# Loads of three pairs on two queues, weights behind the first x, and the second pair transposed before the FFN

## The chip, the cores and the metric

The kernel runs on one core of a Trainium2 chip. A core has TensorE (matmuls, PE in the profile), VectorE (DVE), ScalarE (ACT), GpSimd (POOL) and SyncE (SP); each works through its own instructions in order and they meet by semaphores. Loads and stores go through 16 DMA engines; SP and ACT issue them on hardware queues, GpSimd on a software queue. The metric is the device time of one execution in microseconds (us); lower is better.

## The reference

A state-space scan (Mamba-2 form) is followed by a feed-forward network (FFN). The scan works on x (4 batches, 8 heads, 768 positions, 32 dims), decays a, and B and C with 16 states. Per head, in chunks of positions:

```python
L = np.exp(cum[:, :, :, None] - cum[:, :, None, :]) * causal
M = np.einsum('bhin,bhjn->bhij', Cc, Bc) * L
y = np.einsum('bhij,bhjd->bhid', M, xc) + np.einsum('bhin,bhnd->bhid', Cc, state) * exp(cum)
state = decay_full * state + np.sum(Bx, axis=2)
```

The result, seen as 3072 tokens of 256 features, goes through the FFN with w_in (256 x 2048) and w_out (2048 x 256):

```python
h = np.maximum(x @ w_in, 0.0)
return h * h @ w_out
```

## The kernel before

The work is cut into 12 pairs. A pair is one batch and 256 positions of all 8 heads, two chunks of 128 positions (u = 0, 1); `PAIRS` runs over the four batches first, so that pairs 0 to 3 are the first 256 positions of the four batches. The decays are scanned into prefix products once at the start (`P_sb`, its reciprocal `Pinv`, and the totals `Ptot`), and the factors are multiplied into C and x: C times the prefix product is `cz`, x times its reciprocal is `xs`.

One pair goes through these steps, each a small function: `ph_load` (DMAs of C, B and x; rows of 128 bytes for B and C, 256 for x), `prep_c`, `prep_b`, `prep_x` (`cz`, the bf16 copy `Bb`, and `xs`; `ph_prep` does all three on GpSimd), `ph_tr` (six transposes on TensorE into PSUM, then one copy to `bct`), `ph_mt` (16 matmuls C times B), `ph_mask` (four multiplications by the causal mask on VectorE, into `mts`), `ph_u` (16 matmuls for the chunk's new state), `ph_s` (states S of the two chunks, on VectorE), `ph_y` (40 or fewer matmuls into Y, then the copy to `T`, bf16). For pair 0 the copy to T is split in two, one half on ScalarE and one on VectorE.

A pair's T is one block of 256 tokens of the FFN. A block has eight steps; a step is `mm1` (four 256-column matmuls with w_in, ReLU on ScalarE into `hb`), `square` (VectorE, one step later) and `mm2` (four matmuls with w_out, `LAG` = 4 steps later). `steps` lists all 96 steps. `at(s, fn, ...)` hangs a pair's functions on a step; within a step the order is mm1, dummy matmuls in the first steps, the functions hung there, square, mm2. From pair 4 on the schedule is regular, eight steps a pair. Pairs 1 to 3 have their steps in `first_steps`, as (tr, u, s, mt, four masks, y), and the first 16 steps interleave blocks 0 and 1 (`head`).

The order on every engine is the order in which the code is written out (`manual_schedule`). Before the loop the code goes: the early loads, dummy matmuls (`warm`, which compute nothing that is used), the decay scan, all of pair 0, the preparation of pair 1. The weights come in eight transfers on GpSimd's queue, each a quarter of w_in (`load_wi`, L125) or w_out (`load_wo`, L130), cast to bf16. Three things order the loads:

- the queue: SP issues a, C0, x0, C1, B1, x1, then pairs 2 and later; ACT issues the constants `cf` and B0;
- `touch` copies on GpSimd (L403, L430): a tiny copy whose input is awaited, so that the weight loads behind it in the queue leave later. L403 waits for `P_sb`, L430 for C of pair 2;
- `gate=True` in `ph_load`: GpSimd writes one element of each destination first, so that the DMA waits for GpSimd to get there.

PSUM has three pools of two buffers each: `ps_h` (tag hps: FFN hidden, and in the start U of pair 0), `ps_o` (tag ops: FFN output, dummies, transposes of pair 0), `ps_s` (tag A: the scan). A buffer is taken again when the last reader of its earlier content is done.

Of the kernel before, what the change touches and what calls it, by code (L numbers as in the profile page):

```python
# [30 lines left out]
def kernel(  # L31
# [14 lines left out]
    nc = tc.nc  # L46
# [64 lines left out]
    def ph_load(k, order="CBx", eng=None, gate=False):  # L111
        b, j = PAIRS[k]
        t = loaded.setdefault(k, {})
        for what in order:
            src, w = {"B": (B, N), "C": (C, N), "x": (x, D)}[what]
            dst = nat.tile([128, NH, 2 * w], FP32, tag=f"{what}_nat", name=f"{what}_nat{k}")
            if gate:
                nc.gpsimd.memset(dst[:, 0, 0:1], 0.0)
            (eng or nc.sync).dma_start(  # L119
                out=dst, in_=_dap(src, (b * NH * S + j * 256) * w,  # L120
                                  [[2 * w, 128], [S * w, NH], [1, 2 * w]]))
            t[what] = dst
# [6 lines left out]
    def load_wo(f0, f1):  # L129
        nc.gpsimd.dma_start(  # L130
            out=w_out_b[:, f0:f1, :],
            in_=moe_w_out[f0 * 128:f1 * 128, :].rearrange("(f p) d -> p f d", p=128))
# [24 lines left out]
    def prep_x(k, eng):  # L157
        b, j = PAIRS[k]
        xs = prep.tile([128, 2, 256], BF16, tag="xs", name=f"xs{k}")
        eng.tensor_tensor(  # L160
            out=_fap(xs, 0, [[256, 2], [32, 8], [1, 32]]),
            in0=_fap(loaded[k]["x"], 0, [[32, 2], [64, 8], [1, 32]]),
            in1=_fap(Pinv, b * 24 + j, [[96, 2], [3, 8], [0, 32]]), op=ALU.mult)
        live.setdefault(k, {})["xs"] = xs
# [7 lines left out]

    def ph_tr(k):
        v = live[k]
        pool, tag = (ps_o, "ops") if k < 1 else (ps_s, "A")
        tr = pool.tile([128, 2, 3, 128], BF16, tag=tag, name=f"tr{k}",
                       padded_shape=[128, 2, 4, 128] if k < 1 else [128, 4, 4, 128])
        for r in range(2):
            nc.tensor.transpose(tr[:, r, 0, :], v["Bb"][:, r, :], eye_b)  # L179
            for g in range(2):  # L180
                nc.tensor.transpose(tr[:, r, 1 + g, :], v["cz"][:, r, 112 * g:112 * g + 128], eye_b)  # L181
        bct = big.tile([128, 2, 3, 128], BF16, tag="bct", name=f"bct{k}")
        nc.vector.tensor_copy(out=bct, in_=tr)  # L183
        v["bct"] = bct

    def ph_mt(k):
# [15 lines left out]
    def ph_mask(k, q, src=None):  # L202
        v = live[k]
        nc.vector.tensor_tensor(  # L204
            out=v["mts"][:, q], in0=v["mt"][q // 2][:, q % 2] if src is None else src,
            in1=_fap(cb, 128, [[128, 2], [0, 2], [1, 128]]), op=ALU.mult)
# [157 lines left out]
    with tc.manual_schedule():  # L364
        nc.sync.dma_start(out=a_nat, in_=_dap(a, 0, [[256, 96], [1, 256]]))
        nc.scalar.dma_start(out=cf, in_=cf_d.ap())
        ph_load(0, "C")
        ph_load(0, "B", nc.scalar)
        ph_load(0, "x")
        nc.gpsimd.dma_start(out=cb, in_=cb_d.ap())  # L370
        load_wi(0, 4)
        ph_load(1)

        nc.vector.memset(dum, 0.0)  # L374
        nc.vector.memset(zer, 0.0)
        for i in range(3):
            nc.vector.memset(cz[i], 0.0)
        dps = ps_o.tile([128, 256], FP32, tag="ops", name="dps", padded_shape=[128, 512])

        def warm(n, cols=256):  # L380
            for _ in range(n):
                nc.tensor.matmul(dps[:, 0:cols], dum[:, 0:128], dum[:, 0:cols],  # L382
                                 start=True, stop=True, skip_group_check=True)

        warm(18)
        nc.vector.tensor_scalar(out=a_cl, in0=a_nat, scalar1=1e-6, scalar2=1.0, op0=ALU.max, op1=ALU.min)
        for u in range(2):
            nc.vector.tensor_tensor_scan(out=cp_r[:, u * 128:(u + 1) * 128], data0=a_cl[:, u * 128:(u + 1) * 128],
                                         data1=zer, initial=1.0, op0=ALU.mult, op1=ALU.add)
        nc.vector.tensor_tensor(out=pick_p, in0=_fap(pick, 0, [[0, 2], [1, 12]]),  # L390
                                in1=_fap(cp_r, 127, [[128, 2], [0, 12]]), op=ALU.mult)
        ptr = ps_h.tile([128, 2, 96], FP32, tag="hps", name="ptr", padded_shape=[128, 2, 256])
        for r in range(2):
            nc.tensor.transpose(ptr[:, r, :], _fap(cp_r, r, [[2, 128]]), eye_f)
        warm(1)
        pps = ps_h.tile([128, 2, 12], FP32, tag="hps", name="pps", padded_shape=[128, 2, 256])
        nc.tensor.matmul(pps, spread, pick_p, start=True, stop=True)
        nc.scalar.copy(out=P_sb, in_=ptr)
        prep_b(0, nc.scalar)
        nc.scalar.copy(out=Ptot, in_=pps)  # L400
        prep_c(0, nc.vector)
        nc.vector.reciprocal(out=_fap(Pinv, 0, [[96, 2], [3, 32]]), in_=_fap(P_sb, 0, [[96, 2], [3, 32]]))
        nc.gpsimd.tensor_copy(out=touch, in_=P_sb[:, 0, 0:1])  # L403
        load_wi(4, 8)
        load_wo(0, 4)
        prep_x(0, nc.gpsimd)
        load_wi(8, 12)
        load_wo(4, 8)
        warm(4, 128)
        ph_tr(0)  # L410
        warm(8, 128)
        ph_mt(0)
        warm(6, 128)
        mtc = big.tile([128, 2, 2, 2, 128], BF16, tag="mtc", name="mtc", bufs=1)
        for i in (1, 0):
            nc.scalar.copy(out=mtc[:, i], in_=live[0]["mt"][1][:, i])
        ph_mask(0, 0)
        warm(8, 128)
        ph_u(0)
        warm(8, 128)  # L420
        ph_mask(0, 1)
        ph_mask(0, 3, mtc[:, 1])
        ph_mask(0, 2, mtc[:, 0])
        ph_s(0, (0,))
        prep_b(1, nc.scalar)
        prep_c(1, nc.vector)
        prep_x(1, nc.gpsimd)
        load_wo(8, 12)
        ph_load(2, gate=True)
        nc.gpsimd.tensor_copy(out=touch, in_=loaded[2]["C"][:, 0, 0:1])  # L430
        load_wi(12, 16)
        load_wo(12, 16)
        ph_load(3, gate=True)
        ph_y(0)
        warm(9, 128)
        ph_s(0, (1,))

        head = ([(0, f) for f in range(6)] + [(1, f) for f in range(6)]
                + [(0, 6), (1, 6), (0, 7), (1, 7)])
        steps = head + [(b, f) for b in range(2, NPAIR) for f in range(8)]  # L440
        todo = {}

        def at(s, fn, *args):
            todo.setdefault(max(s, 0), []).append((fn, args))

        def recip_rest():
            nc.vector.reciprocal(out=_fap(Pinv, 1, [[96, 2], [3, 32], [1, 2]]),
                                 in_=_fap(P_sb, 1, [[96, 2], [3, 32], [1, 2]]))

        at(7, recip_rest)  # L450
        first_steps = {
# [3 lines left out]
        for k in range(1, NPAIR):  # L455
            s0 = 8 * k - LEAD
            if k == 2:
                at(8, prep_c, k, nc.gpsimd)
                at(10, prep_b, k, nc.scalar)
                at(9, prep_x, k, nc.gpsimd)  # L460
            elif k == 3:
                at(13, ph_prep, k)
            elif k > 3:
                at(s0 - (8 if k == 4 else 15), ph_load, k)
                at(s0 - (4 if k == 4 else 7), ph_prep, k)
            if k in first_steps:
                tr, uu, st, mt, ms, yy = first_steps[k]
                at(uu, ph_u, k)
            else:
                tr, st, mt, ms, yy = s0, s0 - 1, s0 + 2, (s0 + 2, s0 + 3, s0 + 3, s0 + 4), s0 + 6  # L470
            at(tr, ph_tr, k)
            at(mt, ph_mt, k)
            for q in range(4):
                at(ms[q], ph_mask, k, q)
            at(st, ph_s, k)
            at(yy, ph_y, k)
        for s in range(len(steps) + LAG):
            if s < len(steps):
                mm1(*steps[s])
            if 1 <= s < LAG:  # L480
                warm(4, 128)
            for fn, args in todo.pop(s, []):
                fn(*args)
            if 1 <= s < len(steps) + 1:
                square(*steps[s - 1])
            if LAG <= s < len(steps):
                mm2(*steps[s - LAG])
        mm2_last(NPAIR - 1, [f for _, f in steps[len(steps) - LAG:]])
# [30 lines left out]
```

## Time and profile before

| | |
|---|---|
| median of 13 runs | 126.67 us (125.59 to 128.28) |
| the profiled execution | 127.09 us, its span 125.3 us |
| TensorE busy | 115.4 us, 92% of the span |
| VectorE, ScalarE, GpSimd busy | 85.7, 72.8, 31.8 us |
| granted TensorE clock, mean | 0.979 |
| loads of C, B, x on SP, from issue to landing (median) | 4.0, 4.1, 4.4 us |
| w_in and w_out, a quarter each | 5.6 and 6.3 us |
| first FFN matmul | 11.38 us |
| `ph_mt` of pair 4, 5, 6 | 43.68, 52.40, 61.13 us |

The span runs from the first to the last instruction of the profiled execution; its own time has 1.79 us beside that. "Granted clock" is the share of full speed that TensorE's throttle allowed. A timeline line gives start, duration, engine, line, operation, output and input, count, and in brackets how long the engine had stood still before it and what ended that. A line of the chain of waits gives start, length and the work. A line of the windows gives the stretch and its length, busy time of PE, weight loads, DVE, ACT and POOL with counts, the granted clock, the DMA share and GB/s.

### The profile page before, as it was taken

The page shows a single profiled execution, that of the slowest core. Times are in us where ns is not written, and L with a number is a line of the kernel's source. Part 1 is how long each engine was busy: PE and PEld are TensorE (multiplying, and loading weights), DVE is VectorE, ACT ScalarE, POOL GpSimd, SP SyncE. Part 2 cuts the span into 40 slices and gives each one's busy share as a digit, 9 for nine tenths or more (in the row PEclk, how much of TensorE's full clock was granted, in tenths as well). Part 3 has the DMA queues.
Part 4 walks back from the last instruction along what each step waited for, and adds up shares of the span by engine and source line. Part 5 has one row for each costly group of instructions (what it writes and reads, how often), then busy time and mean ns, then how long its engine had stood idle before and what let it go on. Part 6 is the DMA issues. An engine that isn't in the chain of part 4 may idle for free.

```text
span 125.3 us, 4310 instructions
## 1 busy us (share of the span) xinstructions
PE 115.4 (92%) x1814; PEld 93.0 (74%) x1814; DVE 85.7 (68%) x207; ACT 72.8 (58%) x131; POOL 31.8 (25%) x61
## 2 busy tenths in 40 slices
PE   6779889859999999999999999999999999999970
PEld 4558668636667888788788788887887897788840
DVE  3486896519599798696797794874956947934520
ACT  4244555613557558567485585576575765867720
POOL 5184502803691060250330420602400000000000
PEclk9999999995999999999999999999999999999997
DMA  4999997799854724707505607229020020010211
GB/s 84 200 195 171 193 120 139 75 157 187 156 106 159 130 59 107 148 4 154 102 0 133 123 35 154 67 88 166 8 86 8 0 86 5 14 70 5 84 42 42
DMA packets 42804, 12.10 MB, mean 97 GB/s; under 512 B 37824, under 2 KB 41360, under 8 KB 42784
## 3 DMA queue, kind: packets, MB, share of 16 engines
q1 hardware_dynamic: 38240, 9.28, 34.5%
q0 software_dynamic: 3248, 2.20, 13.4%
q10 hardware_dynamic: 1296, 0.35, 1.7%
q8 instruction: 14, 0.23, 0.8%
q14 instruction: 6, 0.05, 0.1%
HBM read 10.77 MB, written 3.15 MB: 111 GB/s over the span
## 4 chain that ended last, share of the span: by engine, by line
PE 72%; DMA 15%; SPq 4%; DVE 3%; POOL 2%; ACT 1%; issue 1%; DVEq 0%; POOLq 0%
PE ops L336 30%; PE hps L316 29%; DMA x_nat<-in_x_dram 7%; DMA w_in_b<-in_moe_w_in_dram 4%; DMA C_nat<-in_C_dram 4%; SPq L119 3%; PE Y L256 3%; PE mt L193 3%; PE Y L284 2%; PE tr L181 2%; DVE h L326 2%; PE U L222 1%; PE ops L349 1%; DVE mts L204 1%; POOL xs L160 1%
## 5 line engine op out<-in xcount | busy, mean ns | idle before, releaser
L320 ACT ACTIVATE hb<-hps 128x512 bf16<-128x512 f32 x96 | 57.5, 599 | 39.0 <-PE hps L316 38.2
L316 PE MATMUL hps<-T,w_in_b 128*128 128x256 bf16 x384 | 58.6, 276 | 2.8 <-DMA w_in_b<-in_moe_w_in_dram 2.4
L336 PE MATMUL ops<-w_out_b,h 128*128 128x256 bf16 x368 | 56.2, 276 | 0.0
L326 DVE TENSOR_TENSOR h<-hb 128x512 bf16<-128x512 bf16 x96 | 39.7, 437 | 7.4 <-ACT hb L320 7.4
L316 PEld LDWEIGHTS <-w_in_b 128*128 128x128 bf16 x384 | 37.5, 99 | 8.5 <-DMA w_in_b<-in_moe_w_in_dram 2.8
L336 PEld LDWEIGHTS <-h 128*128 128x128 bf16 x368 | 34.0, 99 | 6.5 <-issue 2.0
L204 DVE TENSOR_TENSOR mts<-mt,cb 128x512 bf16<-128x512 f32 x46 | 30.2, 682 | 10.3 <-PE mt L193 10.3
L140 POOL TENSOR_TENSOR cz<-C_nat,P_sb 128x256 bf16<-128x256 f32 x10 | 6.7, 669 | 38.8 <-DMA C_nat<-in_C_dram 23.1
L160 POOL TENSOR_TENSOR xs<-x_nat,Pinv 128x512 bf16<-128x512 f32 x12 | 12.8, 1064 | 8.0 <-DMA x_nat<-in_x_dram 6.8
L183 DVE COPY bct<-tr 128x768 bf16<-128x768 bf16 x12 | 6.7, 557 | 10.4 <-PE tr L181 10.3
L382 PE MATMUL dps<-dum 128*128 128x128 bf16 (+1 forms) x74 | 8.2, 261 | 1.1 <-DVE dum L374 1.1
L382 PEld LDWEIGHTS <-dum 128*128 128x128 bf16 x74 | 6.0, 109 | 2.3 <-DVE dum L374 1.1
L305 ACT CAST T<-Y 128x512 bf16<-128x512 f32 x11 | 6.4, 585 | 0.7 <-PE Y L256 0.3
L361 ACT COPY osb<-ops 128x512 f32<-128x512 f32 x11 | 6.4, 580 | 0.4 <-PE ops L336 0.4
L154 POOL CAST Bb<-B_nat 128x128 bf16<-128x128 f32 x18 | 5.2, 315 | 1.3 <-DMA B_nat<-in_B_dram 1.3
L181 PE MATMUL tr<-cb,cz 128*128 128x128 bf16 x48 | 5.3, 220 | 0.0
L193 PE MATMUL mt<-bct 32*64 32x256 bf16 x192 | 5.1, 280 | 0.2 <-DVE bct L183 0.2
L245 DVE TENSOR_SCALAR S<-z,Ptot 128x64 bf16<-128x64 f32 x16 | 4.7, 296 | 0.6
L179 PE MATMUL tr<-cb,Bb 128*128 128x128 bf16 x24 | 4.8, 220 | 0.3 <-ACT Bb L152 0.3
L256 PE MATMUL Y<-mts,xs 64*32 64x128 bf16 x384 | 5.0, 219 | 0.0
L244 DVE TENSOR_TENSOR z<-U,S 128x64 f32<-128x64 f32 x16 | 3.6, 224 | 1.9 <-PE U L222 1.4
L284 PE MATMUL Y<-bct,S 32*32 32x128 bf16 x160 | 4.4, 217 | 0.2 <-DVE S L241 0.2
(45 smaller groups left out, 45.2 us busy)
## 6 DMA issues: line engine op xcount, KB each, us to landing
x_nat<-in_x_dram SPq DMA_DIRECT2D x12, 256.0 KB, 4.4
out_dram<-osb SPq DMA_DIRECT2D x11, 256.0 KB, 2.6
C_nat<-in_C_dram SPq DMA_DIRECT2D x12, 128.0 KB, 4.0
B_nat<-in_B_dram SPq DMA_DIRECT2D x11, 128.0 KB, 4.1
w_in_b<-in_moe_w_in_dram POOLq DMA_DIRECT2D x4, 256.0 KB, 5.6
w_out_b<-in_moe_w_out_dram POOLq DMA_DIRECT2D x4, 256.0 KB, 6.3
B_nat<-in_B_dram ACTq DMA_DIRECT2D x1, 128.0 KB, 4.8
out_dram<-osb ACTq DMA_DIRECT2D x1, 128.0 KB, 1.7
```

The lines of the kernel that those rows point to most:

```text
L140: eng.tensor_tensor(out=_fap(czk, 0, [[240, 2], [32, 8], [1, 16]]), in0=_fap(loaded[k]["C"], 0, [[16, 2], [32, 8], [1, 16]]), in1=_fap(P_s ...
L160: eng.tensor_tensor(out=_fap(xs, 0, [[256, 2], [32, 8], [1, 32]]), in0=_fap(loaded[k]["x"], 0, [[32, 2], [64, 8], [1, 32]]), in1=_fap(Pinv ...
L181: nc.tensor.transpose(tr[:, r, 1 + g, :], v["cz"][:, r, 112 * g:112 * g + 128], eye_b)
L193: nc.tensor.matmul(mt[q // 2][64 * u:64 * u + 64, q % 2, r, :, :], bct[32 * q:32 * q + 32, r, 0, u * 64:u * 64 + 64], _fap(bct[32 * q:32 * ...
L204: nc.vector.tensor_tensor(out=v["mts"][:, q], in0=v["mt"][q // 2][:, q % 2] if src is None else src, in1=_fap(cb, 128, [[128, 2], [0, 2], ...
L256: nc.tensor.matmul(Y[u][32 * q:32 * q + 32, g, :], v["xs"][64 * u:64 * u + 64, r, h * 32:h * 32 + 32], v["mts"][64 * u:64 * u + 64, q, r, ...
L284: nc.tensor.matmul(Y[u][32 * q:32 * q + 32, g, :], S_b[32 * q:32 * q + 32, g * 32:(g + 1) * 32], _fap(v["bct"][32 * q:32 * q + 32], 128 + ...
L316: nc.tensor.matmul(hps[:, i, :], w_in_b[:, g, f * 128:(f + 1) * 128], T[blk][:, g].rearrange("p r u t -> p (r u t)"), start=(g == 0), stop ...
L320: nc.scalar.activation(out=hb, in_=hps, func=AF.Relu)
L326: nc.vector.tensor_tensor(out=h2, in0=hb, in1=hb, op=ALU.mult)
L336: nc.tensor.matmul(ops[blk][:, r, :], h2[:, i, r * 128:(r + 1) * 128], w_out_b[:, f, :], start=(f == 0 and r == 0), stop=(f == 15), skip_g ...
L382: nc.tensor.matmul(dps[:, 0:cols], dum[:, 0:128], dum[:, 0:cols], start=True, stop=True, skip_group_check=True)
```

## The change

Three places change.

The loads: B and x of pair 1 move from SP's queue to ACT's. The loads of pair 2 follow C of pair 1 on SP at once, with neither gate nor touch. On GpSimd `prep_x(0)` takes the place of the first touch, so that the second weight transfer and all later ones stand behind it; `prep_x(1)` stands behind w_in 8:12, and the last four weight transfers follow it without a touch between them.

Pair 1: `prep_c(1)` on VectorE stands directly behind the copy of pair 0's transposes, `prep_b(1)` on ScalarE behind the copies of pair 0's mt, and `ph_tr(1)` stands before `ph_y(0)`, in a buffer of `ps_h`; ScalarE makes its copy to `bct`. Both states of pair 0 are made before Y.

The steps: pair 1's mt and masks come one step earlier, pair 2's functions four, pair 3's one. `head` interleaves after five steps of block 0 and not six. Pair 2 is prepared whole on GpSimd at step 3. The dummy matmuls change in number.

```diff
     def ph_tr(k):
         v = live[k]
-        pool, tag = (ps_o, "ops") if k < 1 else (ps_s, "A")
+        pool, tag = [(ps_o, "ops"), (ps_h, "hps")][k] if k < 2 else (ps_s, "A")
...
-        nc.vector.tensor_copy(out=bct, in_=tr)
+        if k == 1:
+            nc.scalar.copy(out=bct, in_=tr)
+        else:
+            nc.vector.tensor_copy(out=bct, in_=tr)
...
         load_wi(0, 4)
-        ph_load(1)
+        ph_load(1, "C")
+        ph_load(1, "B", nc.scalar)
+        ph_load(1, "x", nc.scalar)
+        ph_load(2)
...
-        nc.gpsimd.tensor_copy(out=touch, in_=P_sb[:, 0, 0:1])
+        prep_x(0, nc.gpsimd)
         load_wi(4, 8)
         load_wo(0, 4)
-        prep_x(0, nc.gpsimd)
         load_wi(8, 12)
-        load_wo(4, 8)
         warm(4, 128)
         ph_tr(0)
+        prep_c(1, nc.vector)
         warm(8, 128)
         ph_mt(0)
-        warm(6, 128)
+        warm(8, 128)
         mtc = big.tile([128, 2, 2, 2, 128], BF16, tag="mtc", name="mtc", bufs=1)
         for i in (1, 0):
             nc.scalar.copy(out=mtc[:, i], in_=live[0]["mt"][1][:, i])
+        prep_b(1, nc.scalar)
         ph_mask(0, 0)
-        warm(8, 128)
         ph_u(0)
-        warm(8, 128)
+        warm(10, 128)
         ph_mask(0, 1)
         ph_mask(0, 3, mtc[:, 1])
         ph_mask(0, 2, mtc[:, 0])
-        ph_s(0, (0,))
-        prep_b(1, nc.scalar)
-        prep_c(1, nc.vector)
+        ph_s(0)
         prep_x(1, nc.gpsimd)
+        load_wo(4, 8)
         load_wo(8, 12)
-        ph_load(2, gate=True)
-        nc.gpsimd.tensor_copy(out=touch, in_=loaded[2]["C"][:, 0, 0:1])
         load_wi(12, 16)
         load_wo(12, 16)
         ph_load(3, gate=True)
+        ph_tr(1)
         ph_y(0)
         warm(9, 128)
-        ph_s(0, (1,))
-
-        head = ([(0, f) for f in range(6)] + [(1, f) for f in range(6)]
-                + [(0, 6), (1, 6), (0, 7), (1, 7)])
+
+        head = ([(0, f) for f in range(5)] + [(1, f) for f in range(4)]
+                + [(0, 5), (1, 4), (1, 5), (0, 6), (1, 6), (0, 7), (1, 7)])
...
-            1: (0, 3, 4, 1, (1, 1, 2, 2), 5),
-            2: (11, 14, 14, 12, (12, 12, 13, 13), 15),
-            3: (16, 19, 20, 17, (17, 18, 18, 19), 21)}
+            1: (None, 2, 3, 0, (0, 0, 1, 1), 4),
+            2: (7, 10, 10, 8, (8, 8, 9, 9), 11),
+            3: (15, 18, 19, 16, (16, 17, 17, 18), 20)}
...
             if k == 2:
-                at(8, prep_c, k, nc.gpsimd)
-                at(10, prep_b, k, nc.scalar)
-                at(9, prep_x, k, nc.gpsimd)
+                at(3, ph_prep, k)
             elif k == 3:
-                at(13, ph_prep, k)
+                at(11, ph_prep, k)
...
-            at(tr, ph_tr, k)
+            if tr is not None:
+                at(tr, ph_tr, k)
...
-            if 1 <= s < LAG:
-                warm(4, 128)
+            if 2 <= s < LAG:
+                warm(3, 128)
```

More of the change, by code (lines that the diff above doesn't have):

```diff
@@ L174, in ph_tr @@
         v = live[k]
-        pool, tag = (ps_o, "ops") if k < 1 else (ps_s, "A")
+        pool, tag = [(ps_o, "ops"), (ps_h, "hps")][k] if k < 2 else (ps_s, "A")
         tr = pool.tile([128, 2, 3, 128], BF16, tag=tag, name=f"tr{k}",
-                       padded_shape=[128, 2, 4, 128] if k < 1 else [128, 4, 4, 128])
+                       padded_shape=[128, 2, 4, 128] if k < 2 else [128, 4, 4, 128])
         for r in range(2):
```

## The prediction

> **What bounds the kernel now.** I read the page first, then the chain of waits, then windows, then the timeline of the first 45 us.
>
> ```profile
> span 125.3 us, 4310 instructions
> PE 115.4 (92%) x1814; PEld 93.0 (74%) x1814; DVE 85.7 (68%) x207; ACT 72.8 (58%) x131; POOL 31.8 (25%) x61
> PEclk9999999995999999999999999999999999999997
> ```
>
> TensorE sets the time, except in one slice of granted clock, the tenth (28.2 to 31.3 us). In the chain of waits, the matmuls of L193 recur every 8.7 us from 43.68 on with little but matmuls between them: one pair of the steady loop.
>
> ```profile
> 15.76 5.10 DMA C_nat<-in_C_dram
> 21.44 5.13 DMA w_in_b<-in_moe_w_in_dram
> 26.61 0.61 PE hps L316 x4
> ...
> 43.68 0.35 PE mt L193 x16
> ...
> 52.40 0.35 PE mt L193 x16
> ```
>
> The change ends before that loop, so 125.3 - 43.68 = 81.6 us stay and only the instant of `ph_mt(4)` can move. The windows up to it (PE busy is the second figure, granted clock the third from last):
>
> ```profile
> 11.38:18.64 7.26, 6.36 (x123) 4.78 (x124) 5.94 (x15) 4.17 (x7) 2.00 (x5) 1.00 1.14 164
> 18.64:24.61 5.97, 5.97 (x54) 4.88 (x53) 3.23 (x7) 3.87 (x8) 3.44 (x8) 1.00 0.73 111
> 24.61:26.61 2.00, 0.00 (x0) 0.00 (x1) 0.49 (x2) 0.00 (x0) 0.07 (x1) 1.00 1.06 117
> 28.00:31.50 3.50, 3.50 (x34) 2.24 (x32) 3.20 (x8) 1.19 (x2) 1.23 (x4) 0.52 1.00 179
> ```
>
> TensorE stands for 2.00 us, then works 3.5 us at clock 0.52, which loses 0.48 x 3.50 = 1.68 us. The timeline has the reason: the last quarter of w_in is issued at 21.44 because GpSimd's touch copy waited for C_nat2.
>
> ```profile
> 20.98 0.26 POOL L430 COPY touch<-C_nat 128x1 f32<-128x1 f32 x1 [5.18 <-DMA C_nat<-in_C_dram]
> 26.61 0.61 PE L316 MATMUL hps<-T,w_in_b 128*128 128x256 bf16 x4 [2.00 <-DMA w_in_b<-in_moe_w_in_dram]
> ```
>
> **The change, part by part** (pN is pair N; times from the span's start).
>
> *The stall.* The touch and the gate of p2's loads go; p2's loads are issued early on SP, and w_in 12:16 follows the other weights. GpSimd's queue in order: x_nat0 lands at 1.66 + 6.5 = 8.2, `xs0` runs about 8.35 to 9.4 (row: 1.06), then issues of 0.75 each: w_in 4:8 at 9.45, w_out 0:4 at 10.2, w_in 8:12 at 10.95, `xs1` to 12.9, then four more to 16. w_in 12:16 leaves at about 14.4. With the landings of before (4.7 to 6.8 us for a weight) it lands at 19 to 21, and behind its predecessors at their slowest spacing (2.4 us, 13.2 to 15.6) at about 23.5. Step 12, which reads it, comes at about 27.7 (step 6 at 21.3, worked out below, six steps of 8 x 0.109 and 1.2 for p2's tr, mt and U). The 2.00 us go, and with them the cause of the 1.68 us. Next late is nothing of the weights, by little: w_in 4:8 lands at 9.45 + 4.8 = 14.25, used at 15.75; w_in 8:12 at 10.95 + 6.3 = 17.25, used at 17.55. C2, B2 and x2, behind C1 on SP, compete with w_in 4:8 as C1, B1 and x1 did before. The hold itself costs nothing under that cover; without it, 0.5 us (6.8 for w_in 4:8) to 1.6 us (8.2, the longest early landing, for w_in 8:12).
>
> *Where the new wait sits.* `prep_c(1)` moves on VectorE from behind p0's masks to before them. In before:
>
> ```profile
> L119 SPq DMA_DIRECT2D C_nat<-in_C_dram x1: 1004/1004/1004, 2.3 to 2.3; - x1
> DMA to landing us min/median/max: 6.7/6.7/6.7
> 6.89 0.56 DVE L183 COPY bct<-tr 128x768 bf16<-128x768 bf16 x1
> 7.98 1.29 DVE L204 TENSOR_TENSOR mts<-mt,cb 128x512 bf16<-128x512 f32 x2 [0.54 <-PE mt L193]
> 9.19 0.76 DVE L204 TENSOR_TENSOR mts<-mtc,cb 128x512 bf16<-128x512 bf16 x2
> ```
>
> C_nat1 lands at 2.28 + 6.7 = 9.0, while the masks begin at 7.98. VectorE runs in order: masks, S0, half of T0 and the whole FFN now queue behind C_nat1. It still stands behind x_nat0 on SP. Lower bound: 9.0, since what leaves its way (w_in 4:8 and w_out 0:4, issued at 6.33 and 7.04) is replaced by B1 and x1 on ACT. By bytes: about 1454 KB had moved by 9.0; now a, cf, C0, B0, cb, x0, w_in 0:4, C1 (1176 KB), B1 (128) and most of x1 (170 to 256) make 1474 to 1560 KB, at 200 KB/us 9.1 to 9.5. Upper bound: all of B1 and x1 on top at the rates of the steady loop's loads, alone on their queue (about 160 GB/s for B, 0.8 us; 240 for x, 1.1 us): 10.9. I take 9.4, nearest the byte count, because several queues together held 200 GB/s here.
>
> A page bears on this. The Trainium skill ("DMA: Bandwidth & Descriptors", Rules for kernel authors) says that spreading DMAs over SP, ACT and GpSimd saves only issue time, as all share 16 engines. That speaks against a gain from the second queue; the near-equal landings of C0 on SP (3.9 us) and B0 on ACT (4.8 us) agree, and by it C1 would land no earlier than the byte count has it.
>
> *ACT's issues.* SP's first four issues took 0.39, 0.43, 0.58 and 1.00. ACT's four (cf, B0, B1, x1) then end near 3.3, its table load (1.28) at 4.6, before `P_sb` at 5.57. At the worst early row (2.38 for x1) `P_sb` is 0.4 late, hidden behind C_nat1; uncovered, 0.4.
>
> *From C_nat1 to the first FFN matmul.* `prep_c(1)` 9.45 to 9.86 (0.41); four masks as before (7.98 to 9.95) to 11.95; S_0 0.27 to 12.25. `ph_tr(1)` now stands on PE ahead of `ph_y(0)` and takes the "hps" buffer of U0, free only after S_0: tr 0.40, to 12.75; Y0 0.5. ACT copies bct1 ahead of its half of T0: 768 columns, extrapolated from 0.37 (256) and 0.58 (512), are 0.80, 12.95 to 13.75, then T0 0.37; first matmul of step 0 at about 14.25. Before it was 11.38: **+2.87**. Bounds +2.3 (no wait for the buffer, C1 at 9.0) to +4.4 (C1 at 10.9).
>
> *Steps 0 to 5.* tr1 and bct1 are done, so p1's masks start at t0 + 0.95 and run 2.6, two squares 0.84, S 0.27, Y1 at t0 + 4.75, T1, step 5 at 6.15, step 6 at t0 + 7.05. Before, step 6 began at 18.64 = 11.38 + 7.26: **-0.2**. Six dummy matmuls of 0.06 fewer are inside this; the other added ones run in waits. `prep_b(1)` is earlier on ACT, behind the mtc copies, and B_nat1 (9.6 before) is in by then; `ph_prep(2)` is on GpSimd from about 16.3 to 18.6, for step 7 at about 22.
>
> *Steps 6 to 24.* The matmul work is the same. p2 ends at step 11 instead of 15: the 0.28 before `tr2` and the 0.2 for T2 go, while `recip_rest` (0.95), now ahead of bct2 on VectorE, may hold mt2 by 0.2: **-0.3** (0 to -0.5).
>
> *A new cold stretch.* PE is idle 8.35 to 9.45 and, after U0 and ten dummies, 10.25 to 12.35: 2.1 us at a stretch. The row says that 2.00 us idle were followed, 1.3 us after work resumed, by 3.4 us at half clock. Here that lands on tr1, Y0, mm1 and mt1, of which some 1.2 us count, the rest hides behind the masks. Between 0 and 1.2 I take **+0.7**, as the gap equals the row's. The Trainium skill ("TensorE: Matmul & The Clock Gate", Part 1) gives about 3.4 us idle as what cools the clock; the 2.00 us row disagrees, and by the page this term would be 0, the sum 125.8.
>
> **Sum** on the profiled execution (127.09 us; 1.79 lie outside its span): +2.87 - 0.2 - 0.3 - 2.00 - 1.68 + 0.7 = -0.61, 126.5. That execution lies 0.42 above the median, 126.67, so against the median it is -0.2, or -0.15%. Part of the runs may lack the half-clock stretch of before (they spread from 125.59 to 128.28), which is no more than that 0.42.
>
> **Rivals.** A measurement of this kernel tells some 0.5%, 0.63 us: faster is below 126.04, slower above 127.30.
>
> 1. *Clean start.* C_nat1 at 9.0 (-0.4) and no cold stretch (-0.7): 125.4. For it: nothing but the two bounds, and that granted clock stayed 1.00 through the smaller gaps of the first 18 us. Against: the 2.1 us gap.
> 2. *C_nat1 late.* At 10.9: +1.5, 128.0. It decides from a landing of 10.2 on (9.4 and the 0.8 from 126.5 to 127.3). For it: ACT's x1 has 256-byte rows and shares with C1's 128-byte rows packet by packet. Against: 200 GB/s held under several queues.
> 3. *The hold starves step 2 or 4.* w_in 8:12 at 10.95 + 8.2 = 19.15: +1.6, 128.1. For it: x_nat1's 8.2 us under such traffic. Against: weights never took more than 6.8.
> 4. *The stall stays*, w_in 12:16 landing after step 12: needs 27.7 - 14.4 = 13.3 us from issue, no row above 8.2. It would give 128.5 or more.
>
> **Chances.** Forecast 0.42, with its own range 125.7 to 127.4; rival 1 0.24, rival 2 0.19, rival 3 0.12, rival 4 0.03. The forecast lies within the bounds: of its 0.42, 0.17 fall below 126.04, 0.16 within, 0.09 above. With rival 1 (0.23 faster, 0.01 within) and rivals 2 to 4 (0.01 within, 0.33 slower): faster 0.40, same 0.18, slower 0.42. The range reaches from rival 1's value, widened by the 0.4 that the profiled execution lies above the median, to those of rivals 2 and 3 with 0.3 for their partly coming together: 125.0 to 128.4.
>
> **What would show it.** The touch at L430 gone, w_in 12:16 landed before 25 and no idle at step 12; VectorE's `cz1` waiting on C_nat until 9.0 to 10.9; the first L316-type matmul near 14.25; `tr1` right after S_0; a half-clock window between 12 and 17 instead of 28. Most wrong would be a C_nat1 landing under 8, or weights that stop steps 2 to 5.

## The result, and the profile after

The changed kernel takes 128.09 us (median of 11 runs, 127.76 to 129.18), the kernel before 126.42 us (48 runs, 125.22 to 128.28): by the medians 1.67 us or 1.3% slower. The ratio used from here on leaves out executions more than 1.5% above the fastest of their kernel (14 of 48 of before, none of the changed kernel's); it is 1.0162, 95% interval 1.0132 to 1.0191: 1.6% slower. The forecast was 126.5 us, level with before. The time lies inside the stated range, at the place that rival 2 had worked out (128.0), but the loss is clear of noise.

The page of the changed kernel, its head and the row of granted clock:

```profile
span 126.5 us, 4281 instructions
PE 114.6 (91%) x1804; PEld 93.0 (74%) x1804; DVE 86.8 (69%) x206; ACT 73.0 (58%) x130; POOL 32.3 (26%) x58
PEclk9998559999999999999999999999999999999996
```

The half-clock slice at 28 us is gone. In its place two and a half slices, from 9.5 to 19 us, are low. The chain of waits of the changed kernel (start, length, work) shows what the beginning now runs on:

```profile
2.28 7.99 DMA C_nat<-in_C_dram
...
10.63 3.18 DVE mts L207 x4
...
16.82 0.85 PE hps L319 x4
17.67 0.66 PE mt L196 x16
18.33 2.46 DVE mts L207 x4
...
44.84 0.35 PE mt L196 x16
```

C of pair 1 lands at 10.27, and pair 0's four masks, which never needed it, begin at 10.63 and take 3.18 us. In the chain of before there was no C of pair 1 at all, and the masks ended at 9.95. The timeline of the changed kernel over the same stretch:

```profile
10.29 0.43 DVE L140 TENSOR_TENSOR cz<-C_nat,P_sb 128x256 bf16<-128x256 f32 x1 [2.73 <-DMA C_nat<-in_C_dram]
...
10.63 1.28 DVE L207 TENSOR_TENSOR mts<-mt,cb 128x512 bf16<-128x512 f32 x2
...
11.37 0.72 POOL L125 DMA_DIRECT2D w_in_b<-in_moe_w_in_dram  x1
11.83 1.98 DVE L207 TENSOR_TENSOR mts<-mtc,cb 128x512 bf16<-128x512 bf16 x2
12.09 1.09 POOL L160 TENSOR_TENSOR xs<-x_nat,Pinv 128x512 bf16<-128x512 f32 x1
...
14.06 0.27 PE L179 MATMUL tr<-cb,Bb 128*128 128x128 bf16 x1 [3.18 <-DVE S L244]
...
16.61 1.06 PE L319 MATMUL hps<-T,w_in_b 128*128 128x256 bf16 x4
...
44.77 0.42 PE L196 MATMUL mt<-bct 32*64 32x256 bf16 x16
```

VectorE stands for 2.73 us on C. The two masks with bf16 input take 1.98 us where before's took 0.76: one of them 0.41, the other 1.65, with GpSimd's `xs` of pair 1 running beside it. TensorE stands for 3.18 us ahead of pair 1's transposes. The first FFN matmul starts at 16.61 (before: 11.38), and four matmuls take 1.06 us and not 0.60. The issue at 11.37 is that of w_in 8:12. From `ph_mt(4)` to the end it is 81.7 us, as before (81.6), if both are taken from the chain of waits (44.84 here, 43.68 before), which counts a piece from the end of the one before it. The windows of the changed kernel (TensorE busy second, granted clock third from last):

```profile
9.50:12.00 2.50, 0.92 (x26) 0.76 (x26) 1.71 (x4) 0.50 (x2) 2.50 (x4) 0.94 1.18 142
12.00:18.60 6.60, 4.54 (x78) 2.93 (x78) 3.25 (x7) 1.67 (x3) 6.37 (x13) 0.51 1.15 169
18.60:24.00 5.40, 4.44 (x90) 3.32 (x89) 4.54 (x12) 3.14 (x6) 0.00 (x0) 1.00 1.54 207
24.00:44.77 20.77, 20.33 (x328) 16.41 (x325) 17.52 (x40) 13.00 (x23) 7.85 (x13) 1.00 0.60 117
```

Two things are to be seen: a stretch at half clock where the masks, the transposes and the first FFN steps lie, and from 24 us on a TensorE that is busy for 20.33 of 20.77 us. No FFN matmul waits for a weight any more, so the stall at step 12 is gone, as the change says. The whole loss lies before 24 us. The clock of 0.94 in the first window and 0.51 in the second puts the half clock at 11.7 to 18.5. TensorE's last matmul before the gap ended at 10.88, so the clock fell 0.8 us into the gap of 3.18 us and not behind it.

### The profile page after: what moved, and what is told of

Its sections match the earlier page's. It is cut to its first block, busy times and chain, and to the rows that moved or that the text cites. A ratio compares the mean times of both kernels' runs of the same rounds, so it can differ in the third digit from the quotient of the medians.

```text
span 126.5 us, 4281 instructions
## 1 busy us (share of the span) xinstructions
PE 114.6 (91%) x1804; PEld 93.0 (74%) x1804; DVE 86.8 (69%) x206; ACT 73.0 (58%) x130; POOL 32.3 (26%) x58
## 4 chain that ended last, share of the span: by engine, by line
PE 79%; DVE 9%; DMA 6%; ACT 1%; SPq 1%; issue 1%; DVEq 0%
PE ops L339 32%; PE hps L319 31%; DVE mts L207 6%; DMA C_nat<-in_C_dram 6%; PE Y L259 4%; PE mt L196 3%; PE Y L287 3%; PE tr L181 2%; DVE h L329 1%; PE tr L179 1%; PE ops L352 1%; PE U L225 1%; PE dps L388 1%; SPq L119 1%; DVE S L244 0%
## 5 line engine op out<-in xcount | busy, mean ns | idle before, releaser
L339 PE MATMUL ops<-w_out_b,h 128*128 128x256 bf16 x368 | 55.5, 273 | 0.0
L329 DVE TENSOR_TENSOR h<-hb 128x512 bf16<-128x512 bf16 x96 | 40.9, 452 | 6.9 <-ACT hb L323 6.9
L160 POOL TENSOR_TENSOR xs<-x_nat,Pinv 128x512 bf16<-128x512 f32 x12 | 12.9, 1077 | 12.5 <-DMA x_nat<-in_x_dram 10.4
L186 DVE COPY bct<-tr 128x768 bf16<-128x768 bf16 x11 | 6.1, 557 | 9.4 <-PE tr L181 9.4
L154 POOL CAST Bb<-B_nat 128x128 bf16<-128x128 f32 x20 | 6.1, 334 | 1.5 <-DMA B_nat<-in_B_dram 0.8
L181 PEld LDWEIGHTS <-cz 128*128 128x128 bf16 x48 | 3.8, 101 | 3.4 <-issue 3.3
L287 PEld LDWEIGHTS <-S 32*32 32x32 bf16 x160 | 2.3, 91 | 3.7 <-issue 1.9
## 6 DMA issues: line engine op xcount, KB each, us to landing
C_nat<-in_C_dram SPq DMA_DIRECT2D x12, 128.0 KB, 4.1
B_nat<-in_B_dram SPq DMA_DIRECT2D x10, 128.0 KB, 4.0
B_nat<-in_B_dram ACTq DMA_DIRECT2D x2, 128.0 KB, 6.3
```

What stands on the lines that cost most here:

```text
L160: eng.tensor_tensor(out=_fap(xs, 0, [[256, 2], [32, 8], [1, 32]]), in0=_fap(loaded[k]["x"], 0, [[32, 2], [64, 8], [1, 32]]), in1=_fap(Pinv ...
L287: nc.tensor.matmul(Y[u][32 * q:32 * q + 32, g, :], S_b[32 * q:32 * q + 32, g * 32:(g + 1) * 32], _fap(v["bct"][32 * q:32 * q + 32], 128 + ...
L329: nc.vector.tensor_tensor(out=h2, in0=hb, in1=hb, op=ALU.mult)
L339: nc.tensor.matmul(ops[blk][:, r, :], h2[:, i, r * 128:(r + 1) * 128], w_out_b[:, f, :], start=(f == 0 and r == 0), stop=(f == 15), skip_g ...
```

## The experiments

The accounts to be told apart. *The masks' wait* (rival 2): pair 0's masks and all behind them queue on VectorE behind C of pair 1, and the idle TensorE goes cold. *The held weights* (rival 3): `prep_x(0)` ahead of the second weight transfer makes the weights late. *GpSimd beside the masks*: `xs` of pair 1 is what makes the bf16 mask slow. And, for the gain that was forecast, *what the stall was worth* in an ordinary execution of the kernel before. All ratios are to the kernel before on the same chip; the three profiles of the kernel before have spans of 123.9 to 125.3 us, so single profiles differ by more than 1 us, and where a ratio and a profile differ, the ratio decides.

**C of pair 1 behind the masks.** The changed kernel, with `prep_c(1)` on VectorE after pair 0's states.

```diff
         ph_tr(0)
-        prep_c(1, nc.vector)
         warm(8, 128)
...
         ph_s(0)
+        prep_c(1, nc.vector)
         prep_x(1, nc.gpsimd)
```

> The changed kernel with one thing undone: prep_c(1) on VectorE stands behind pair 0's masks and states and no longer ahead of them. My theory (the masks of pair 0 wait for C of pair 1, which cost most of the loss): masks from about 8.1 to 10.1 us, no bf16 mask beside xs1, first FFN matmul at about 13.3 instead of 16.55. Then the held weights become the wait: w_in 8:12 lands near 18.9, and step 4 would want it at 16.6, so about 1 us of the 3.2 is given back: some 2 us off the changed kernel, 126 us, about level with before. Rival (it is the late weights or the loads themselves that set the start, the masks only stand in line with them): the first FFN matmul moves, but step 5 stays near 23.1 and the time stays at 128.

Measured: ratio 1.0154 (1.0062 to 1.0246), median of four executions 127.59 us (the kernel before beside it: 126.68). Its timeline:

```profile
7.85 1.29 DVE L207 TENSOR_TENSOR mts<-mt,cb 128x512 bf16<-128x512 f32 x2 [0.54 <-PE mt L196]
...
9.06 1.04 DVE L207 TENSOR_TENSOR mts<-mtc,cb 128x512 bf16<-128x512 bf16 x2
...
13.20 1.06 PE L319 MATMUL hps<-T,w_in_b 128*128 128x256 bf16 x4
...
18.85 0.61 PE L319 MATMUL hps<-T,w_in_b 128*128 128x256 bf16 x4 [1.54 <-DMA w_in_b<-in_moe_w_in_dram]
```

The masks' wait is real: without it they begin at 7.85, and the first FFN matmul comes 3.4 us earlier, at 13.20. But 1.54 of that is at once spent at step 4, on w_in 8:12, which GpSimd issued at 10.95 and which landed 7.9 us later, at 18.8. That is rival 3, hidden in the changed kernel only because everything was later still. The half clock still comes, for one slice of its page (12.5 to 15.6 us) in place of two and a half. The profiled execution is the fastest of its four (126.45 us); over the four the ratio has gained nothing that can be measured. That is a weak statement: by the medians the loss is 0.91 us and not 1.67, and four executions cannot tell the two readings apart.

**`xs` of pair 1 last on GpSimd.** The changed kernel, with the weights issued first.

```diff
         ph_s(0)
-        prep_x(1, nc.gpsimd)
         load_wo(4, 8)
         load_wo(8, 12)
...
         load_wo(12, 16)
+        prep_x(1, nc.gpsimd)
         ph_load(3, gate=True)
```

> The changed kernel with prep_x(1) moved on GpSimd from behind w_in 8:12 to behind the last weight issue (w_out 12:16), so that no GpSimd arithmetic runs beside pair 0's masks. Theory (the bf16 mask that took 1.65 us in place of 0.41 was held by GpSimd's xs1 at 12.09 to 13.18): all four masks take 2.0 us and not 3.2, the first FFN matmul comes at 15.3, the time falls by about 1.2 us to 126.9. Rival (the mask is slowed by the DMA traffic or by the weights' issuing on GpSimd): a bf16 mask of over 1 us remains, and the time stays at 128.

Measured: ratio 1.0164 (1.0102 to 1.0226), median of four executions 128.09 us (before: 126.68). Timeline:

```profile
10.78 0.42 DVE L140 TENSOR_TENSOR cz<-C_nat,P_sb 128x256 bf16<-128x256 f32 x1 [3.46 <-DMA C_nat<-in_C_dram]
...
11.65 1.52 POOL L130 DMA_DIRECT2D w_out_b<-in_moe_w_out_dram  x2
...
12.32 1.57 DVE L207 TENSOR_TENSOR mts<-mtc,cb 128x512 bf16<-128x512 bf16 x2
```

So `xs` is not the only thing that was seen beside a slow mask. With `xs` out of the way until 14.60, one bf16 mask still took 1.24 us and the other 0.41, now beside two weight issues of GpSimd. It is the only such mask: in the next experiment both bf16 masks took 0.41 us beside a weight issue. C landed at 10.75 here, 0.5 later than in the changed kernel's profile.

**B and x of pair 1 back on SP.** The changed kernel with one queue for pair 1.

```diff
-        ph_load(1, "C")
-        ph_load(1, "B", nc.scalar)
-        ph_load(1, "x", nc.scalar)
+        ph_load(1)
         ph_load(2)
```

> The changed kernel with B and x of pair 1 back on SP behind C of pair 1, all else as changed (weights still held, masks still behind prep_c(1)). Theory (the second queue lets B1 and x1 take turns with C1, which is what moved its landing from 9.0 to 10.27): C1 lands at 8.6 to 9.0, the masks end near 11.2 before xs1 begins, the first FFN matmul at about 14, the time at 125.5 to 126.5. Rival (the DMA engines' total rate decides, not the queue; or C1's place behind x0): C1 lands at 10 or later again and the time stays within 0.6 of 128.

Measured: ratio 1.0156 (1.0076 to 1.0235), median of four executions 127.92 us (before: 126.68). Timeline:

```profile
8.90 0.48 DVE L140 TENSOR_TENSOR cz<-C_nat,P_sb 128x256 bf16<-128x256 f32 x1 [1.58 <-DMA C_nat<-in_C_dram]
...
10.50 0.75 DVE L207 TENSOR_TENSOR mts<-mtc,cb 128x512 bf16<-128x512 bf16 x2
10.55 0.72 POOL L125 DMA_DIRECT2D w_in_b<-in_moe_w_in_dram  x1
...
14.04 0.83 PE L319 MATMUL hps<-T,w_in_b 128*128 128x256 bf16 x4
...
19.39 0.61 PE L319 MATMUL hps<-T,w_in_b 128*128 128x256 bf16 x4 [1.71 <-DMA w_in_b<-in_moe_w_in_dram]
```

On one queue C of pair 1 lands at 8.87, 1.4 us before the 10.27 that it needs with B and x beside it on ACT. So in these profiles (a single one of them has one queue) the second queue delays the load that everything waits for. The time expected of it, 125.5 to 126.5 us, did not come. The gain goes the same way as in the first experiment: the first FFN matmul is 2.6 us earlier, and w_in 8:12 (issued at 10.55, landed 8.8 us later) then holds step 4 for 1.71 us, after which TensorE runs at half clock once more, from 21 to 25 us.

**The weights not held.** The changed kernel with the touch of `P_sb` back before the second weight transfer; the masks still wait for C.

```diff
-        prep_x(0, nc.gpsimd)
+        nc.gpsimd.tensor_copy(out=touch, in_=P_sb[:, 0, 0:1])
         load_wi(4, 8)
         load_wo(0, 4)
+        prep_x(0, nc.gpsimd)
         load_wi(8, 12)
```

> The changed kernel with only the hold undone (tiny copy of P_sb, then w_in 4:8 and w_out 0:4, then xs0); the masks still stand behind prep_c(1). Theory (the masks' wait is the first of two in line): C1 lands as late or later, since weights take turns with it, the first FFN matmul stays at 16.5 or comes later, no matmul waits for a weight, the time stays at 128 to 128.5. Rival (the hold is the cause): the time falls by 1 us or more.

Measured: ratio 1.0166 (1.0024 to 1.0307), median of four executions 128.69 us (before: 126.62). Timeline:

```profile
10.81 0.42 DVE L140 TENSOR_TENSOR cz<-C_nat,P_sb 128x256 bf16<-128x256 f32 x1 [3.32 <-DMA C_nat<-in_C_dram]
...
12.35 0.75 DVE L207 TENSOR_TENSOR mts<-mtc,cb 128x512 bf16<-128x512 bf16 x2
...
15.90 1.06 PE L319 MATMUL hps<-T,w_in_b 128*128 128x256 bf16 x4
```

C lands at 10.8, against 10.27 in the changed kernel but 10.75 in the second experiment, where the weights are held; so it is not shown that the early weights take anything from it. With GpSimd idle beside them the bf16 masks are at 0.75 us again, so the first FFN matmul is 0.7 earlier in sum. From 26 to 46 us its TensorE then stands for 1.36 us, the changed kernel's for 0.44. Nothing is gained in the ratio.

**Both together.** C behind the masks and the weights not held: the first and the fourth diff in one kernel. The rest of the change (two queues, pair 2 early, no touch before the last quarter) stays.

> Two things of the changed kernel undone: prep_c(1) behind pair 0's masks (as in the run that moved it alone), and the weights no longer held: the tiny copy of P_sb ahead of w_in 4:8 and w_out 0:4 again, xs0 behind them. Theory (the masks' wait and the late weights are two waits of nearly the same length, one behind the other, so that undoing one alone shows the other: 1.5 us for w_in 8:12 at step 4): w_in 8:12 lands near 17, step 4 waits under 0.5 us, step 5 starts near 20 us (20.8 with the masks moved alone, 23.1 in the changed kernel), the time is 125.5 to 126.5, level with before or a little under. Rival (the hold costs nothing, the rest of the loss is the cold clock or pair 1's early transposes): the time stays at 127.5, as with the masks moved alone.

Measured: ratio 0.9993 (0.9929 to 1.0057), median of ten executions 126.31 us (before: 126.62), no FFN matmul waiting for a weight. Timeline:

```profile
8.96 0.75 DVE L207 TENSOR_TENSOR mts<-mtc,cb 128x512 bf16<-128x512 bf16 x2
...
11.96 0.42 DVE L140 TENSOR_TENSOR cz<-C_nat,P_sb 128x256 bf16<-128x256 f32 x1
...
14.66 0.60 PE L319 MATMUL hps<-T,w_in_b 128*128 128x256 bf16 x4
```

The two edits together give the loss back, while either alone gives back nothing that can be measured. The interval lies below that of the changed kernel and, by 0.0005, below that of the first experiment; that of the fourth overlaps it, so on that side the statement rests on the medians, 126.31 against 128.69. That both together remove the loss is therefore shown; that neither does alone rests on four executions each. The profiles do not add to it: this one and that of the first experiment are level by then, with `ph_mt(4)` at 42.92 and 42.71. C of pair 1 lands at 11.4 here, but VectorE reaches `cz` of pair 1 only at 11.96, so nothing waits for the landing. Nor is the half clock gone: it holds from 10.8 to 14.2 us in this profile, half as long as in the changed kernel.

**The hold alone, on the kernel before.** Two kernels. In one, the touch of pair 2's C is left out of the kernel before; in the other, that and `prep_x(0)` in place of the touch of `P_sb`.

```diff
         ph_load(2, gate=True)
-        nc.gpsimd.tensor_copy(out=touch, in_=loaded[2]["C"][:, 0, 0:1])
         load_wi(12, 16)
```

> The kernel before without the touch copy at L430, nothing else: w_in 12:16 leaves when GpSimd reaches it, at about 15.8, and no longer after C2 has landed. Theory (the stall of 2.0 us and the half clock after it are worth 3 to 3.7 us by themselves): w_in 12:16 lands near 21, step 12 does not wait, the time is 123 to 123.7. Rival (the touch protects pair 2's loads: without it C2 and x2 come later, the transposes of pair 2 at step 11 wait, and the gain is given back): a wait of 1 to 2 us moves to pair 2's cz or tr near 23 us and the time is 125.5 to 126.5.

```diff
-        nc.gpsimd.tensor_copy(out=touch, in_=P_sb[:, 0, 0:1])
+        prep_x(0, nc.gpsimd)
         load_wi(4, 8)
         load_wo(0, 4)
-        prep_x(0, nc.gpsimd)
         load_wi(8, 12)
```

> The kernel before without its copy at L430 (as in the run without that touch, 125.8 us) and with the weights held as in the changed kernel: xs0 ahead of w_in 4:8 and w_out 0:4, in place of the copy of P_sb. All loads of pair 0 and 1 as before, masks not behind C1. Theory (holding the weights by 3 us moves w_in 8:12 to about 18 us where step 4 wants it at 15.2): the wait at step 4 grows from 1.9 to about 3, the time rises by 0.7 to 1.3 to about 126.8. Rival (small packets out of the way first make everything land earlier): w_in 8:12 lands no later, the time is 125.8 or less.

Measured: without the touch 0.9938 (0.9887 to 0.9989), median 125.82 us (before: 126.68), one of ten executions, of 224.07 us, aside; with the hold as well 1.0102 (0.9987 to 1.0218), median of four executions 127.49 us (before: 126.62). The 123 to 123.7 us that the theory expected without the touch were missed: the stall at step 12 is gone, but in its profile step 4 waits for w_in 8:12.

```profile
17.10 0.61 PE L316 MATMUL hps<-T,w_in_b 128*128 128x256 bf16 x4 [1.93 <-DMA w_in_b<-in_moe_w_in_dram]
```

The table of waits of the kernel with the hold (who waits for whom, the total in us, how often, the longest):

```profile
PE hps L316 <- DMA w_in_b<-in_moe_w_in_dram: 3.1, 2, 2.2
```

Between the two points the hold costs some 1.6%, though the intervals touch. By the 0.9994 of the kernel without the touch, measured a second time below, it is 1.1%. The 3.1 us are 0.95 at step 2 and 2.17 at step 4, with half clock behind them, in an execution that was the longest of its four (128.70 us). The prediction had costed the hold at nothing under cover of a late start and at 0.5 to 1.6 us without it.

**More dummies.** The changed kernel with 60 dummy matmuls and not 10 behind U of pair 0, so that TensorE stays busy while the masks wait.

```diff
         ph_u(0)
-        warm(10, 128)
+        warm(60, 128)
         ph_mask(0, 1)
```

> The changed kernel with 60 instead of 10 dummy matmuls behind pair 0's U, which fill TensorE's wait of 3.2 us for pair 1's transposes. Theory (that idle stretch is what halves the granted clock from 11.7 to 18.6 us, and the half clock costs tr1, Y0, the dummies, mm1 and mt1 about 1.2 us before pair 1's masks begin): granted clock 1.00 throughout, the first FFN matmul at 15.6 to 15.9 in place of 16.55, the time lower by 0.9 to 1.4: 126.7 to 127.2. Rival (the half clock is hidden behind VectorE's masks): granted clock 1.00 and the time still within 0.4 of 128.1.

Measured: ratio 1.0075 (1.0027 to 1.0123), median of ten executions 126.99 us (before: 126.62). The row of granted clock on its page:

```profile
PEclk9999999999999999999999999999999999999999
```

And its timeline:

```profile
11.49 1.05 POOL L160 TENSOR_TENSOR xs<-x_nat,Pinv 128x512 bf16<-128x512 f32 x1 [0.63 <-DMA x_nat<-in_x_dram]
11.62 1.55 DVE L207 TENSOR_TENSOR mts<-mtc,cb 128x512 bf16<-128x512 bf16 x2
...
15.10 0.60 PE L319 MATMUL hps<-T,w_in_b 128*128 128x256 bf16 x4
```

The clock stays full and 0.9% comes back: the half-clock stretch costs about 1.1 us, (1.0162 - 1.0075) x 126.4. It is the only single edit of the changed kernel whose interval lies below the changed kernel's. The rest of the loss remains, and so does the slow mask beside `xs` (1.21 us).

**What the stall was worth.** Twice more the kernel without the touch: unchanged, measured a second time, and once with w_in 8:12 issued ahead of w_out 0:4, to take the wait at step 4 away as well.

```diff
         load_wi(4, 8)
-        load_wo(0, 4)
-        prep_x(0, nc.gpsimd)
         load_wi(8, 12)
+        prep_x(0, nc.gpsimd)
+        load_wo(0, 4)
         load_wo(4, 8)
```

> The kernel before without its copy at L430, once more, for comparison with the reordered weights on the same chip. The first time it gave 0.994 of before, with an interval that reached 0.999. Theory: again 0.990 to 0.998. Rival (the touch makes no difference): 1.000 within 0.3%.

> The kernel before without its copy at L430, and with w_in 8:12 issued ahead of w_out 0:4 (and ahead of xs0). Theory (the weights arrive in the order of issue, at a rate that nothing in the order changes, and step 4's wait of 1.9 us is for w_in 8:12 as third in line): w_in 8:12 lands near 15, w_out 0:4 near 17, where the first second-layer matmul wants it at about 17.3; step 4 waits under 0.3 us, step 5 of block 1 starts near 18.7 in place of 19.9, the time is 124.5 to 125, 1.2 to 1.7% under before. Rival (the DMA engines are full until 17 us, so that what was third is late wherever it stands): w_out 0:4 becomes the wait, and the time equals that of the run without the touch, 0.5% under before.

Measured: without the touch again 0.9994 (0.9951 to 1.0038); with the other order too 0.9966 (0.9928 to 1.0005), where 124.5 to 125 us, 1.2 to 1.7% under before, had been expected. The table of waits of the kernel without the touch, from its second profile:

```profile
PE tr L179 <- ACT Bb L152: 1.5, 1, 1.5
...
PE hps L316 <- DMA w_in_b<-in_moe_w_in_dram: 0.3, 1, 0.3
```

Of the kernel with the other order too:

```profile
PE tr L179 <- ACT Bb L152: 1.8, 2, 1.6
```

The stall at step 12 is gone in all of them, and another of 1.5 to 1.9 us has come: before pair 2's transposes here, since B of pair 2 now lands late among the weights (in the second kernel 8.5 us after its issue at 16.23), and at step 4 for w_in 8:12 in the first profile without the touch. By the two measurements, taking the touch away is worth 0.0 to 0.6%, net of the wait that comes instead, and not 3.68 us. What the stall at step 12 is worth where no other wait takes its place, no run here separates.

**The kernel before, profiled twice more.**

> The kernel before, unchanged, one more look. Theory (the 2.0 us stall for w_in 12:16 is always there, but the half clock after it depends on where the idle falls and is not in every execution, so the profiled execution of 127.09 us was one of the slower ones and the term of -3.7 us was too large): a stall of 1.5 to 2.3 us at step 12, and granted clock 1.00 in at least one of the two looks, with a time of 125.5 to 126.3 where it is 1.00. Rival (the half clock follows every time, and the spread of the times comes from elsewhere): half clock for some 3.4 us in both.

> The same kernel before, a second look, with the same expectations: stall of 1.5 to 2.3 us at step 12 in both; granted clock 1.00 in at least one by the theory, half clock in both by the rival.

Measured: 125.72 and 126.94 us. The first one's timeline at step 12:

```profile
26.09 0.61 PE L316 MATMUL hps<-T,w_in_b 128*128 128x256 bf16 x4 [1.20 <-DMA w_in_b<-in_moe_w_in_dram]
```

And the second's:

```profile
26.36 0.61 PE L316 MATMUL hps<-T,w_in_b 128*128 128x256 bf16 x4 [1.44 <-DMA w_in_b<-in_moe_w_in_dram]
```

The stall is 1.20 and 1.44 us, not 2.00 and below the 1.5 that was expected, and the granted clock is 1.000 and 0.997 with no half-clock slice. Of the 56 executions of the kernel before that were timed beside the experiments, 50 had a mean granted clock of 0.991 or more; six had 0.981 to 0.986, about what one half-clock stretch of 3.5 us takes off a span of 125. Their median is 127.5 us, that of the 50 126.45. The profile that the prediction was made from (0.979) was one of the few. All twelve executions of the changed kernel have 0.964 to 0.973, what two such stretches take.

## Why the prediction was wrong

The sum said -0.61 us from profiled execution to profiled execution; it was 128.27 - 127.09 = +1.18. Step by step, by the instants of the changed kernel's profile:

| step | predicted | measured |
|---|---|---|
| C of pair 1 lands | 9.4 (9.0 to 10.9) | 10.27 |
| pair 0's four masks, in sum | 2.1 us | 3.18 us |
| first FFN matmul | 14.25 | 16.61 |
| step 6, with the cold stretch | 22.0 | 23.96 |
| step 6 to `ph_mt(4)` | 21.06 us | 20.88 us |
| `ph_mt(4)`, from the chain | 43.07 | 44.84 |

1. **The first FFN matmul, +2.87: the step that failed.** It was +5.23. The mechanism was the one described (masks behind C of pair 1, transposes of pair 1 behind the states), but the sizes were off: 0.87 for the landing, 1.1 for the masks, 0.5 for what follows S_0, which ran at half clock, less 0.1. (The sum also slips by 0.1: from 9.86, masks as before, 1.97 us, end at 11.83 and not 11.95.) The byte count at 200 GB/s gave 9.1 to 9.5 for C; with B and x of pair 1 on the second queue it came at 10.05 to 10.8 us in the four profiles in which VectorE waits for it with two queues in use, and at 8.87 with one. The upper end, 10.9, was the better guide. The mask row of before (0.41 us each) was taken from a place where `xs` of pair 0 was just ending; moved 2 us, the mask met `xs` of pair 1 and took 1.65.

2. **-2.00 and -1.68, the stall and the half clock: taken from one execution.** Against that profile both terms are right, step 12 no longer waits. Against an ordinary execution they are too large: 1.20 and 1.44 us of stall and no half clock. From step 6 (18.95 and 18.97) to `ph_mt(4)` (42.30 and 43.22 in the chain) those two profiles took 23.35 and 24.25 us; the changed kernel's 20.88 is 2.5 and 3.4 us less, where the terms -0.3, -2.00 and -1.68 had promised 3.98. In the kernel before, with only the touch taken away, the ratio moves by 0.0 to 0.6%, since another wait comes. The prediction let the 0.42 us between profile and median stand for the difference. That is why the medians are further apart (+1.67) than the two profiles (+1.18): the profile of before lies 0.67 above its median in the 48 runs, that of after 0.18 above.

3. **The hold, costed at nothing: a cover that was a second loss.** w_in 8:12 was to land at 17.25 and landed at 18.9 (issue at 11.37 and not 10.95, 7.5 us to landing and not 6.3). In the changed kernel it hides behind the late start, as the text said; take the late start away and the wait is there, 1.54 us in one kernel and 1.71 in another. Rivals 2 and 3 were priced as alternatives, with 0.3 us for both; they are two waits of like length in parallel, and the profiles of the experiments on each alone show how the one hides the other; the times that go with them rest on four executions each.

4. **The cold stretch, +0.7.** It came and was longer, 6.8 us at half clock and not 3.4, and it began inside the gap of 3.18 us and not 1.3 us behind it. The dummies price it at about 1.1 us.

5. **Right:** ACT's four issues end at 3.8 and `P_sb` is not late; steps 0 to 24 came within 0.4 us of their terms; w_in 12:16 lands at 23.1, long before step 12; the loop from `ph_mt(4)` on did not change. Rival 4 is out. Rival 2, with its point of decision at a landing of 10.2, met a landing of 10.27 and a time of 128.09 against its 128.0; part of that agreement is chance, since the masks and not only the landing made up the difference.

The Trainium skill ("DMA: Bandwidth & Descriptors", Rules for kernel authors) says that spreading loads over issuing engines brings no bandwidth. The profiles agree: from 2 to 10 us the DMA engines moved 207 GB/s with the second queue in use and 202 without it. They go further: C landed 1.4 us later with it.

What stays open: what held the one bf16 mask of 1.24 us in the second experiment, which had only weight issues beside it. Every other slow one had `xs` beside it. How the loss divides between the masks' wait, the hold and the half clock is open too, since four executions of an edit cannot tell less than about 1%. Nor was it tried which of the smaller moves (pair 2 four steps earlier, fewer dummies) gives or takes anything in the kernel with both edits; together they are worth nothing that its interval can tell from zero. Nothing here beats the kernel before for certain: the best, the kernel without the touch and with w_in 8:12 first, has 0.9966 with an interval up to 1.0005.

## What to carry to other kernels

Before an instruction that waits for a load is moved ahead of work that does not need it on an in-order engine, price the whole queue behind it at the late end of the landing, not at the byte count: where the DMA engines are full, one load's landing moved by 1.4 us with what went beside it. Where several late loads bound a start together, undoing one can change little and seem to acquit it; undo them together. And before a stall is credited as a gain, look at more than one execution: of three profiles of the kernel before, one had the stall of 2.00 us with a half clock behind it, and two a smaller stall without one.

## What the runs showed of the hardware that was not expected

- A VectorE mask with two bf16 inputs in SBUF took 0.41 us alone and up to 1.65 us beside GpSimd's `xs`; in six profiles (the changed kernel, the first experiment, the one with more dummies, the one with the hold alone, and both further profiles of before) the first such mask ended 0.27 to 0.30 us after that `xs` did. The masks that read PSUM kept 0.68 to 0.69 us. The Trainium skill ("SBUF — State Buffer", the section on who interferes with whom) has VectorE and GpSimd share one pair of ports under an exclusive lock, and says that a VectorE instruction with two SBUF inputs contends with a GpSimd instruction that reads SBUF; `xs` is one, and these ends agree. The 1.24 us beside weight issues alone are not covered by it.
- The half clock did not follow the length of the gap alone. In the kernel before, 2.00 us without a matmul were followed by 3.4 us at half clock in one profile, 1.20 and 1.44 us by none in two others; 1.93 us at step 4 of the kernel without the touch were followed by none, 1.71 us at step 4 of the kernel with one queue by 3.4. In the changed kernel the clock fell 0.8 us into a gap and stayed at half for 6.8. The Trainium skill ("TensorE: Matmul & The Clock Gate", Part 1) names an idle window of about 3.4 us; on these rows less is enough.
- The same transfer in the same program did not land at the same time: w_in 8:12 of the kernel without the touch came at 17.1 in one profile and at 15.9 in the other, on another chip (7.9 and 6.5 us after its issue), and 1.93 us of stall at step 4 came with the first and 0.35 with the second.
